# The second MoE: an earlier weight split and a second fixed slot for the second early expert

## The chip, the cores and the metric

One Trainium2 chip, one of its cores. The metric is the device time of one execution in microseconds; lower is better. The engines are TensorE (PE, matmul; its weight loads are shown as PEld), VectorE (DVE), ScalarE (ACT), GpSimd (POOL) and SyncE (SP); each has its own in-order queue, and DMAs are issued from the queues of ACT, SP and POOL.

## The reference

Clustered attention, a dense MoE layer, and a routed MoE layer. The work that is changed lies in the last one.

```
x = attn(q, k, v, centroids)                     # 2 x 8 heads, 768 tokens each, head size 64 -> [1536, 512]
x = (s * relu(x @ w_in)**2 + b) @ w_out           # 512 -> 2048 -> 512
logits = x @ w_gate                               # 8 experts
e = argmax(logits);  gate = softmax(logits)[e]
out[t] = gate[t] * (relu(x[t] @ w1[e]) @ w2[e])   # w1: 512 x 1024, w2: 1024 x 512, float32
```

## The kernel before

float32 products are made of float16 pairs: an operand is split into hi and lo parts, and three matmuls (hi·hi, hi·lo, lo·hi) are summed. So the weights of an expert, 4 MiB of float32, must be loaded into the four staging tiles stg0 to stg3 (1 MiB each; two for w1, two for w2) and split into a *set* of float16 tiles: ACT writes the hi part (L598), DVE the lo part from it (L599), in eight pieces of 128x1024 on each engine. There are three sets: `wa`, and the tiles `wi` and `wo`, which hold the dense layer's weights until these are done with.

The first MoE ends with a router: each token's row is scattered to the region of its expert in `yreg` (DRAM). The second MoE then works in *slots* of 128 rows of one expert. A slot is a gather of rows by POOL (L636), a transposing DMA by SP (L640, tile x2t), gemm1 with 96 matmuls of 128 columns (L659) into two PSUM halves hps, for each half a relu on ACT (L663) and the lo part on DVE (L664), gemm2 with 24 matmuls of 512 columns (L673), a scaling on ACT (L678, tile o) and a scatter by POOL (L679). The names below are in the order of execution:

- T0, T1, T2: three slots of the expert that has most tokens when the last quarter of the tokens is not yet routed (set wa). They are laid beside the end of the first MoE.
- H1, H2, H3: a fourth slot of that expert (wa), one of expert 1 (wi) and one of expert 0 (wo); `FIRST = (1, 0)` are the two early experts, whose weights are loaded without waiting for the routing (`w_static`, on ACT's queue). Experts 1 and 0 are fixed in the program, the expert of T and H1 and all counts come from the data.
- D0 to D9: ten dynamic slots, on wa, wi, wo in turn. What they work on (expert, rows) is computed by DVE when all tokens are routed, by some 40 small instructions that end with `idx` (L809). Their weights are loaded by SP (L625 and L630); a load is left out at run time where the expert is that of the slot ahead, since the staging tiles still hold it. The split is made again for each slot.
- `USUAL = 10, 11` (L67): ten slots are unconditional; one more stands in a conditional block, the last five of 16 in a block inside it. These run only if the count of slots needed, n_left, is over 10.

The staging tiles have one buffer each, so the load of the next expert's piece waits for the DVE split of that piece. In program order a slot j is followed by the w1 split for slot j+3 (`split(j + 3, 0, ...)`, placed after relu and lo of slot j) and by the w2 split for slot j+2 (`split(j + 2, 1, ...)`, placed after the scaling o of the slot ahead). Which instruction stands where in each engine's queue is settled when the kernel is built, by a scheduler with its own model of durations; it knows nothing of loads that are left out at run time. `tc.issue_after(x)` puts what follows behind x on x's own engine.

The weights of expert 0 are split into wo (L810 and L811) behind two instructions: `st8["relu"]`, the last relu of T2, on ACT, and `idx`, the end of the index computation, on DVE.

Of the kernel before, what the change touches and what calls it, by code (L numbers as in the profile page):

```python
# [7 lines left out]
F32 = mybir.dt.float32  # L8
F16 = mybir.dt.float16
I32 = mybir.dt.int32  # L10
U32 = mybir.dt.uint32
AF = mybir.ActivationFunctionType
ALU = mybir.AluOpType
# [12 lines left out]
SW = 64.0  # L26
# [17 lines left out]
def tile_kernel(ctx: ExitStack, tc, q, k, v, centroids, w_in, w_out, s, b, w_gate, w1, w2, out, dbg=None):  # L44
    nc = tc.nc
# [5 lines left out]
    P = 128  # L51
# [9 lines left out]
    NF = 3  # L61
# [5 lines left out]
    USUAL = 10, 11  # L67
# [524 lines left out]
    def w_split(ws, parts=range(4)):  # L592
        for i in parts:
            hi = ws[:, 2 * (i // 2), (i % 2) * 2048:(i % 2 + 1) * 2048]
            lo = ws[:, 2 * (i // 2) + 1, (i % 2) * 2048:(i % 2 + 1) * 2048]
            for n in range(2):
                a, z = n * 1024, (n + 1) * 1024
                st8["hi"] = nc.scalar.activation(out=hi[:, a:z], in_=stg[i][:, a:z], func=AF.Copy, scale=SW)  # L598
                nc.vector.scalar_tensor_tensor(out=lo[:, a:z], in0=stg[i][:, a:z], scalar=SW, in1=hi[:, a:z],  # L599
                                               op0=ALU.mult, op1=ALU.subtract)  # L600
# [10 lines left out]
    NG = 3  # L611
# [99 lines left out]
    for e in FIRST:  # L711
        nc.vector.tensor_scalar(out=done[:, e:e + 1], in0=done[:, e:e + 1], scalar1=float(P), scalar2=None, op0=ALU.add)
# [20 lines left out]
    hts = [gemm1(sets[0], pre[0][0], (st8["py"], st8["py"])), gemm1(sets[0], pre[1][0], (st8["py"], st8["ps8"]))]  # L733

# [9 lines left out]
    sinv = sp.tile([P, E], F32, name="sinv")  # L744
    sidx = sp.tile([P, E], I32, name="sidx")
    nc.vector.tensor_tensor(out=sinv, in0=doner, in1=nps, op=ALU.is_ge)
    nc.vector.tensor_scalar(out=sinv, in0=sinv, scalar1=OOB, scalar2=None, op0=ALU.mult)
    last = nc.vector.tensor_tensor(out=sidx, in0=doneg, in1=sinv, op=ALU.add)
# [7 lines left out]
    fst = [(pidxi, pinv)] + [(sidx[:, e:e + 1], sinv[:, e:e + 1]) for e in FIRST]  # L756
    fst = [fetch(ygs[(NF + n) % NG], *x) for n, x in enumerate(fst)]
# [52 lines left out]
    with tc.issue_after(st8["relu"].ins), tc.issue_after(last.ins):  # L810
        w_split(sets[2])  # L811
# [4 lines left out]
    def slots(j0, j1, head):  # L816
# [20 lines left out]
        xts = {j: fst[j + len(fst)] for j in head}  # L837
# [12 lines left out]
        for j in (*head, *range(j0, j1)):  # L850
            xt, gate, oid = xts.pop(j)
            ht = gemm1(sets[j % 3], xt)
            if due[1] > j0:
                load(due[1], 2)
            split(j + 3, 0, st8["relu"], st8["hlo"])
            if pend is not None:
                gemm2(*pend)
            split(j + 2, 1, *([st8["o"]] if "o" in st8 else []))
# [5 lines left out]
    slots(0, USUAL[0], range(-len(fst), 0))  # L864
# [29 lines left out]
```

## Time and profile before

| what | value |
|---|---|
| three runs | 734.92, 737.85, 738.41 us (median 737.85) |
| the profiled execution | 740.1 us, of which its span is 738.4 us |
| PE busy | 654.7 us, 89% of the span |
| DVE, ACT, POOL busy | 525.0, 436.2, 293.5 us |
| DMA | 98.33 MB, 133 GB/s over the span |

The page gives busy times and their share in 40 slices of the span; the timeline gives each engine's instructions in order, merged where alike, with the idle time ahead of each and what released it. Times of the trace count from the span's start. The second MoE's slots take the span from about 540 us to its end.

### The profile page before, as it was taken

How to read it: one execution, taken by the hardware profiler on the slowest of the kernel's cores; microseconds unless marked ns; L12 is line 12 of the kernel's file. 1: busy time of each engine (PE TensorE's matmuls, PEld its weight loads, DVE VectorE, ACT ScalarE, POOL GpSimd, SP SyncE). 2: the span in 40 equal slices, each digit the busy share in tenths (PEclk: the TensorE clock that was granted, in tenths of full speed). 3: DMA queues.
4: the chain of work that ended last, by engine and by line, in shares of the span. 5: the costliest groups of instructions: out<-in, count | busy, mean ns of one | idle time of the engine just before them, and what ended most of it. 6: DMA issues, size and time to landing. Idle time of an engine off the chain costs nothing. (4 is left out here: it accounts for less than half of the span.)

```text
span 738.4 us, 16238 instructions
## 1 busy us (share of the span) xinstructions
PE 654.7 (89%) x6261; PEld 426.1 (58%) x6261; DVE 525.0 (71%) x1109; ACT 436.2 (59%) x897; POOL 293.5 (40%) x336
## 2 busy tenths in 40 slices
PE   2487888898877889999999999999999999998884
PEld 2255666676544545666655654565485776675651
DVE  7999798776899976588832661377844768777672
ACT  6477676777676745567734450156514568667562
POOL 6448576656666564644433300020013234331001
PEclk9998689999899999999999999999999999999898
DMA  8967666662563604430113400038933588789821
GB/s 235 185 158 154 146 169 145 154 133 54 141 158 95 150 25 99 107 70 7 34 13 67 85 15 1 15 110 260 373 101 100 127 270 270 163 270 255 258 101 52
DMA packets 122963, 98.33 MB, mean 133 GB/s; under 512 B 98812, under 2 KB 104956, under 8 KB 120576
## 3 DMA queue, kind: packets, MB, share of 16 engines
q1 hardware_dynamic: 112784, 65.64, 36.5%
q10 hardware_dynamic: 6576, 22.06, 9.4%
q0 software_dynamic: 3520, 9.54, 3.8%
q8 instruction: 51, 0.84, 0.5%
q14 instruction: 32, 0.26, 0.1%
HBM read 85.05 MB, written 7.39 MB: 125 GB/s over the span
## 5 line engine op out<-in xcount | busy, mean ns | idle before, releaser
L291 POOL TENSOR_TENSOR pl<-p,ph 128x384 f16<-128x384 f32 x128 | 128.4, 1011 | 116.4 <-ACT ph L288 58.7
L435 PE MATMUL ps<-xt,wi 128*128 128x384 f16 x768 | 135.3, 330 | 5.7 <-DMA xt<-xp 4.1
L449 PE MATMUL py<-wo,g 128*128 128x512 f16 x576 | 132.2, 382 | 0.0
L283 ACT ACTIVATE p<-st 128x384 f32<-128x384 f32 x192 | 94.1, 491 | 52.5 <-PE st L280 41.8
L242 DVE TENSOR_REDUCE mxt<-sm 128x1 f32<-128x384 f32 x192 | 102.3, 546 | 25.1 <-PE sm L239 24.5
L435 PEld LDWEIGHTS <-wi 128*128 128x128 f16 x768 | 74.5, 99 | 56.2 <-issue 10.4
L449 PEld LDWEIGHTS <-g 128*128 128x128 f16 x576 | 55.2, 98 | 64.0 <-issue 3.7
L239 PE MATMUL sm<-tk 80*128 80x384 f16 x192 | 64.5, 363 | 17.1 <-DVE mxt L242 11.9
L278 PE MATMUL st<-tk 128*128 128x384 f16 x192 | 65.6, 342 | 7.4 <-ACT ph L288 4.6
L288 ACT ACTIVATE ph<-st 128x384 f16<-128x384 f32 x144 | 70.9, 492 | 1.1 <-PE pv L270 1.1
L679 POOL DMA_INDIRECT out<-o,oid x16 | 26.9, 1682 | 103.4 <-ACT o L678 94.6
L280 PE MATMUL st<-qb,tk 128*128 128x384 f16 x192 | 65.8, 343 | 0.0
L673 PEld LDWEIGHTS <-ht 128*128 128x128 f16 x384 | 36.8, 98 | 44.5 <-issue 3.3
L441 ACT ACTIVATE g<-r,b 128x384 f16<-128x384 f32 x64 | 39.4, 618 | 37.1 <-DVE r L440 36.8
L442 DVE SCALAR_TENSOR_TENSOR g<-r,b,g 128x384 f16<-128x384 f32 x64 | 44.8, 701 | 21.3 <-ACT g L441 21.3
L270 PEld LDWEIGHTS <-ph 128*128 128x128 f16 x864 | 45.0, 99 | 20.9 <-issue 4.2
L270 PE MATMUL pv<-v,ph 128*128 128x65 f16 x864 | 52.0, 195 | 5.4 <-ACT ph L288 3.2
L516 POOL DMA_INDIRECT yreg<-yp,posi x12 | 12.8, 1069 | 106.6 <-DVE posi L502 86.1
L599 DVE SCALAR_TENSOR_TENSOR wa<-stg,wa 128x1024 f16<-128x1024 f32 x40 | 46.8, 1218 | 7.7 <-ACT wa L598 7.6
L659 PE MATMUL hps<-x2t,wa 128*128 128x128 f16 x768 | 45.7, 219 | 3.8 <-DVE wa L599 1.5
L659 PEld LDWEIGHTS <-wa 128*128 128x128 f16 x768 | 43.7, 98 | 6.8 <-issue 2.0
L440 DVE SCALAR_TENSOR_TENSOR r<-r,s 128x384 f32<-128x384 f32 x64 | 43.4, 678 | 4.2 <-ACT r L438 4.0
(216 smaller groups left out, 1248.0 us busy)
## 6 DMA issues: line engine op xcount, KB each, us to landing
stg<-in_moe_w SPq DMA_DIRECT2D x44, 1024.0 KB
raw<-in_moe_w_out ACTq DMA_DIRECT2D x16, 512.0 KB
stg<-in_moe_w ACTq DMA_DIRECT2D x8, 1024.0 KB
raw<-in_moe_w_in ACTq DMA_DIRECT2D x10, 512.0 KB
kqv<-in_k SPq DMA_DIRECT2D x16, 192.0 KB
kqv<-in_q SPq DMA_DIRECT2D x16, 192.0 KB
kqv<-in_v SPq DMA_DIRECT2D x16, 192.0 KB
raw<-in_moe_w_in SPq DMA_DIRECT2D x6, 512.0 KB
```

Source lines behind the costliest of these rows:

```text
L239: nc.tensor.matmul(out=sm, lhsT=tk2[0:64 + C, 1, c0 + c, :], rhs=tk2[0:64 + C, 0, n * HC:(n + 1) * HC, :].rearrange("p c x -> p (c x)"), s ...
L242: nc.vector.tensor_reduce(out=mxt[:, c, n:n + 1], in_=sm, axis=AX.X, op=ALU.max)
L270: nc.tensor.matmul(out=pv[:, c, :], lhsT=p[:, c * P:(c + 1) * P], rhs=w, start=first[0], stop=(kc == NC - 1 and c == HC - 1 and p is parts ...
L278: nc.tensor.matmul(out=st.rearrange("p (c x) -> p c x", c=HC), lhsT=tk1[:, kc, 0, :], rhs=tk1[:, c0:c0 + HC, 1, :], start=True, stop=False)
L280: nc.tensor.matmul(out=st, lhsT=tk2[:, 0, kc, :], rhs=qb.rearrange("p c x -> p (c x)"), start=False, stop=True)
L283: nc.scalar.activation(out=p32, in_=st, func=AF.Exp, scale=1.0 / 8.0)
L288: nc.scalar.activation(out=ph, in_=st, func=AF.Exp, scale=1.0 / 8.0)
L291: eng.tensor_tensor(out=pl, in0=p32, in1=ph, op=ALU.subtract)
L435: nc.tensor.matmul(out=ps, lhsT=wi[:, a, kk, f * P:(f + 1) * P], rhs=xt[:, c, kk], start=(kk == 0 and n == 0), stop=(kk == KD - 1 and n == 2))
L449: st8["py"] = nc.tensor.matmul(out=ps, lhsT=g[:, a, f, c * P:(c + 1) * P], rhs=wo[:, w, f], start=(f == 0 and n == 0), stop=(f == KF - 1 a ...
L599: nc.vector.scalar_tensor_tensor(out=lo[:, a:z], in0=stg[i][:, a:z], scalar=SW, in1=hi[:, a:z], op0=ALU.mult, op1=ALU.subtract)
L659: nc.tensor.matmul(out=ps[:, j], lhsT=ws[:, w, kk * F + f0:kk * F + f0 + P], rhs=xt[:, a, kk], start=(i == 0), stop=(i == 3 * KD - 1))
```

## The change

The split of expert 0's weights is traced with two separate orders: its ACT half comes behind the last relu of T1 (`early`), its DVE half behind `idx` as before. The gathers of the H slots are traced after it. Expert 0 gets two fixed slots in a row on the same set wo: H3 with its first 128 rows (in the code -4, the `twin`) and H4 with rows 128 to 255 (in the code -1); no split is traced behind H3 for the slot three further on, since H4 needs none. `done`, from which the table of dynamic slots is made, is raised by 128 more for expert 0. `USUAL` becomes 9, 11: nine dynamic slots D0 to D8 unconditional, two in the first conditional block, five in the second.

```diff
-    USUAL = 10, 11
+    USUAL = 9, 11
@@
-    def w_split(ws, parts=range(4)):
+    def w_split(ws, parts=range(4), hi_after=None, lo_after=None):
...
-                st8["hi"] = nc.scalar.activation(out=hi[:, a:z], in_=stg[i][:, a:z], func=AF.Copy, scale=SW)
-                nc.vector.scalar_tensor_tensor(out=lo[:, a:z], in0=stg[i][:, a:z], scalar=SW, in1=hi[:, a:z],
-                                               op0=ALU.mult, op1=ALU.subtract)
+                with tc.issue_after(hi_after.ins) if hi_after else nullcontext():
+                    nc.scalar.activation(out=hi[:, a:z], in_=stg[i][:, a:z], func=AF.Copy, scale=SW)
+                with tc.issue_after(lo_after.ins) if lo_after else nullcontext():
+                    nc.vector.scalar_tensor_tensor(out=lo[:, a:z], in0=stg[i][:, a:z], scalar=SW, in1=hi[:, a:z],
+                                                   op0=ALU.mult, op1=ALU.subtract)
@@
-    for e in FIRST:
+    second = sp.tile([P, E], F32, name="second")
+    nc.vector.tensor_scalar(out=second, in0=doner, scalar1=float(P), scalar2=None, op0=ALU.add)
+    secondg = sp.tile([P, E], F32, name="secondg")
+    nc.vector.tensor_scalar(out=secondg, in0=doneg, scalar1=float(P), scalar2=None, op0=ALU.add)
+    for e in (*FIRST, FIRST[-1]):
@@
+    early = st8["relu"]
@@
-    nc.vector.tensor_tensor(out=sinv, in0=doner, in1=nps, op=ALU.is_ge)
+    nc.vector.tensor_tensor(out=sinv[:, 0], in0=doner, in1=nps, op=ALU.is_ge)
+    nc.vector.tensor_tensor(out=sinv[:, 1], in0=second, in1=nps, op=ALU.is_ge)
...
-    last = nc.vector.tensor_tensor(out=sidx, in0=doneg, in1=sinv, op=ALU.add)
+    nc.vector.tensor_tensor(out=sidx[:, 0], in0=doneg, in1=sinv[:, 0], op=ALU.add)
+    nc.vector.tensor_tensor(out=sidx[:, 1], in0=secondg, in1=sinv[:, 1], op=ALU.add)
@@
-    with tc.issue_after(st8["relu"].ins), tc.issue_after(last.ins):
-        w_split(sets[2])
+    w_split(sets[2], hi_after=early, lo_after=last)
+
+    fst = [(pidxi, pinv)] + [(sidx[:, n, e:e + 1], sinv[:, n, e:e + 1]) for n, e in ((0, FIRST[0]), (0, FIRST[1]), (1, FIRST[1]))]
+    fst = [fetch(ygs[(NF + n) % NG], *x) for n, x in enumerate(fst)]
@@
+            twin = j == -4
...
-            split(j + 3, 0, st8["relu"], st8["hlo"])
+            if not twin:
+                split(j + 3, 0, st8["relu"], st8["hlo"])
...
-            split(j + 2, 1, *([st8["o"]] if "o" in st8 else []))
+            if j != -1:
+                split((-1 if twin else j) + 2, 1, *([st8["o"]] if "o" in st8 else []))
@@
-    slots(0, USUAL[0], range(-len(fst), 0))
+    slots(0, USUAL[0], (-3, -2, -4, -1))
```

How the instructions then stand in the queues shows at three places. In the rows a number behind a name tells buffers apart, `wo` is the set of expert 0, and `x2` means two pieces.

ACT, from the relus of T1 on. Before:

```order
L663 ACTIVATE ht_8435<-hps_8436 128x512
L663 ACTIVATE ht_8435<-hps_8487 128x512
L663 ACTIVATE ht_8540<-hps_8541 128x512
L663 ACTIVATE ht_8540<-hps_8592 128x512
L678 ACTIVATE o_8668<-yps_8643,gate_7671 128x512
L598 ACTIVATE wo_2954<-stg0_6974 128x1024 x2
L598 ACTIVATE wo_2954<-stg1_6975 128x1024 x2
L598 ACTIVATE wo_2954<-stg2_6976 128x1024 x2
L598 ACTIVATE wo_2954<-stg3_6977 128x1024 x2
L678 ACTIVATE o_8698<-yps_8673,gate_7680 128x512
```

The same place now:

```order
L665 ACTIVATE ht_8440<-hps_8441 128x512
L665 ACTIVATE ht_8440<-hps_8492 128x512
L599 ACTIVATE wo_2954<-stg0_6974 128x1024 x2
L599 ACTIVATE wo_2954<-stg1_6975 128x1024 x2
L599 ACTIVATE wo_2954<-stg2_6976 128x1024 x2
L599 ACTIVATE wo_2954<-stg3_6977 128x1024 x2
L665 ACTIVATE ht_8545<-hps_8546 128x512
L665 ACTIVATE ht_8545<-hps_8597 128x512
L680 ACTIVATE o_8673<-yps_8648,gate_7676 128x512
L680 ACTIVATE o_8703<-yps_8678,gate_7685 128x512
```

The eight hi splits moved from behind T2's relus and T0's scaling to right behind T1's relus.

DVE, from the last index instructions on; yg0 to yg2 are the three gather buffers in turn, and ht_8540 (ht_8545) is T2's. Before:

```order
L809 TENSOR_TENSOR idx_8837<-t3_8838,inv_8834 128x16
L642 TENSOR_SCALAR gate_9356<-yg0_6993 128x1
L645 TENSOR_TENSOR oid_9358<-yg0_6993,inv_8834 128x1
L664 SCALAR_TENSOR_TENSOR ht_8540<-hps_8541,ht_8540 128x512
L642 TENSOR_SCALAR gate_9536<-yg1_6995 128x1
L645 TENSOR_TENSOR oid_9538<-yg1_6995,inv_8834 128x1
L664 SCALAR_TENSOR_TENSOR ht_8540<-hps_8592,ht_8540 128x512
L599 SCALAR_TENSOR_TENSOR wo_2954<-stg0_6974,wo_2954 128x1024 x2
L599 SCALAR_TENSOR_TENSOR wo_2954<-stg1_6975,wo_2954 128x1024 x2
L599 SCALAR_TENSOR_TENSOR wo_2954<-stg2_6976,wo_2954 128x1024 x2
L599 SCALAR_TENSOR_TENSOR wo_2954<-stg3_6977,wo_2954 128x1024 x2
```

Now:

```order
L816 TENSOR_TENSOR idx_8817<-t3_8818,inv_8814 128x16
L601 SCALAR_TENSOR_TENSOR wo_2954<-stg0_6974,wo_2954 128x1024 x2
L601 SCALAR_TENSOR_TENSOR wo_2954<-stg1_6975,wo_2954 128x1024 x2
L601 SCALAR_TENSOR_TENSOR wo_2954<-stg2_6976,wo_2954 128x1024
L647 TENSOR_TENSOR oid_8853<-yg1_6995,sinv_8758 128x1
L644 TENSOR_SCALAR gate_8860<-yg2_6997 128x1
L601 SCALAR_TENSOR_TENSOR wo_2954<-stg2_6976,wo_2954 128x1024
L647 TENSOR_TENSOR oid_8862<-yg2_6997,sinv_8758 128x1
L601 SCALAR_TENSOR_TENSOR wo_2954<-stg3_6977,wo_2954 128x1024 x2
L644 TENSOR_SCALAR gate_8869<-yg0_6993 128x1
L647 TENSOR_TENSOR oid_8871<-yg0_6993,sinv_8758 128x1
L666 SCALAR_TENSOR_TENSOR ht_8545<-hps_8546,ht_8545 128x512
```

The eight lo splits moved ahead of T2's two lo instructions, which now stand behind the splits and behind the gate of the fourth gather (yg0, the second rows of expert 0); behind them comes the gate of D0's gather.

ACT at the end of the slots: the last dynamic slots' splits against the scalings o. Before, from the first piece of D8's w1 (wo, stg0) to that of D9's (wa, stg0 and stg1):

```order
L598 ACTIVATE wo_2954<-stg0_6974 128x1024 x2
L678 ACTIVATE o_10729<-yps_10704,gate_10436 128x512
L598 ACTIVATE wo_2954<-stg1_6975 128x1024 x2
L598 ACTIVATE wi_73<-stg2_6976 128x1024 x2
L663 ACTIVATE ht_10751<-hps_10752 128x512
L598 ACTIVATE wi_73<-stg3_6977 128x1024 x2
L663 ACTIVATE ht_10751<-hps_10803 128x512
L598 ACTIVATE wa_6978<-stg0_6974 128x1024 x2
L678 ACTIVATE o_10879<-yps_10854,gate_10596 128x512
L598 ACTIVATE wa_6978<-stg1_6975 128x1024 x2
```

Now, from the relus of D7 to the scaling of D7; D8 is the last unconditional slot:

```order
L665 ACTIVATE ht_10720<-hps_10721 128x512
L665 ACTIVATE ht_10720<-hps_10772 128x512
L599 ACTIVATE wo_2954<-stg0_6974 128x1024 x2
L599 ACTIVATE wo_2954<-stg1_6975 128x1024 x2
L680 ACTIVATE o_10848<-yps_10823,gate_10565 128x512
L599 ACTIVATE wi_73<-stg2_6976 128x1024 x2
L665 ACTIVATE ht_10862<-hps_10863 128x512
L599 ACTIVATE wi_73<-stg3_6977 128x1024 x2
L665 ACTIVATE ht_10862<-hps_10914 128x512
L599 ACTIVATE wo_2954<-stg2_6976 128x1024 x2
L680 ACTIVATE o_10990<-yps_10965,gate_10716 128x512
L599 ACTIVATE wo_2954<-stg3_6977 128x1024 x2
```

Before, the scaling o stands between the two pieces of the w1 split of D8 and of D9 (and of D7, not shown); now both pieces of D8's w1 stand ahead of it, and a scaling stands only between the two pieces of D8's w2.

## Rows read from the trace of the kernel before

**Rows 1.** Busy time by stretch: engines, granted clock, DMA share, GB/s; the late slots.

```profile
680.00:700.00 20.00, 16.06 (x151) 12.29 (x152) 15.12 (x14) 12.28 (x15) 1.40 (x2) 0.83 0.84 261
```

**Rows 2.** Timeline of PE, a regular pair: start, us, group; the next gemm1's start.

```profile
657.15 5.52 PE L659 MATMUL hps<-x2t,wo 128*128 128x128 f16 x96
...
667.69 5.52 PE L659 MATMUL hps<-x2t,wa 128*128 128x128 f16 x96
```

**Rows 3.** Timeline of PE, slots D7, D8, D9 to the last matmuls.

```profile
678.23 0.83 PE L659 MATMUL hps<-x2t,wi 128*128 128x128 f16 x12
680.17 0.40 PE L659 MATMUL hps<-x2t,wi 128*128 128x128 f16 x4 [1.10 <-ACT wi L598]
...
682.57 5.93 PE L659 MATMUL hps<-x2t,wi 128*128 128x128 f16 x74 [0.63 <-DVE wi L599]
688.34 5.34 PE L673 MATMUL yps<-wa,ht 128*128 128x512 f16 x24
693.51 0.83 PE L659 MATMUL hps<-x2t,wo 128*128 128x128 f16 x12
...
702.98 5.34 PE L673 MATMUL yps<-wi,ht 128*128 128x512 f16 x24
708.16 0.83 PE L659 MATMUL hps<-x2t,wa 128*128 128x128 f16 x12
...
716.64 5.34 PE L673 MATMUL yps<-wo,ht 128*128 128x512 f16 x24
...
726.41 2.53 PE L673 MATMUL yps<-wa,ht 128*128 128x512 f16 x11 [0.88 <-DVE wa L599]
```

**Rows 4.** Timeline of PE, T2's gemm2 and two earlier waits.

```profile
569.05 5.34 PE L673 MATMUL yps<-wa,ht 128*128 128x512 f16 x24
...
580.29 5.52 PE L659 MATMUL hps<-x2t,wi 128*128 128x128 f16 x96 [0.70 <-DVE ht L664]
...
613.90 5.71 PE L659 MATMUL hps<-x2t,wi 128*128 128x128 f16 x96 [1.13 <-DVE ht L664]
```

**Rows 5.** Timeline of ACT while PE starts D7.

```profile
678.48 0.69 ACT L678 ACTIVATE o<-yps,gate 128x512 f32<-128x512 f32 x1 [2.43 <-issue]
679.07 1.99 ACT L598 ACTIVATE wi<-stg 128x1024 f16<-128x1024 f32 x2
```

**Rows 6.** Timeline of ACT ahead of the split of expert 0.

```profile
563.66 1.09 ACT L663 ACTIVATE ht<-hps 128x512 f16<-128x512 f32 x2 [10.42 <-PE yps L673]
...
565.21 7.68 ACT L598 ACTIVATE wo<-stg 128x1024 f16<-128x1024 f32 x8
```

**Rows 7.** Timeline of DVE from idx to the split of expert 0.

```profile
561.43 0.17 DVE L809 TENSOR_TENSOR idx<-t,inv 128x16 int32<-128x16 f32 x1
...
568.15 0.68 DVE L664 SCALAR_TENSOR_TENSOR ht<-hps,ht 128x512 f16<-128x512 f32 x1
...
570.47 9.16 DVE L599 SCALAR_TENSOR_TENSOR wo<-stg,wo 128x1024 f16<-128x1024 f32 x8
```

**Rows 8.** Timeline of POOL, gathers and scatters, and of DVE, a gather's landing.

```profile
565.16 1.00 POOL L636 DMA_INDIRECT yg<-yreg,idx  x1 [6.71 <-DMA x2t<-yg]
...
577.35 1.99 POOL L679 DMA_INDIRECT out<-o,oid  x1 [2.52 <-DMA out<-o,oid]
585.51 1.24 POOL L636 DMA_INDIRECT yg<-yreg,idx  x1 [6.17 <-DMA x2t<-yg]
...
616.96 5.17 POOL L679 DMA_INDIRECT out<-o,oid  x1 [11.17 <-ACT o L678]
...
591.99 0.15 DVE L642 TENSOR_SCALAR gate<-yg 128x1 f32<-128x1 f32 x1 [4.82 <-DMA yg<-yreg,idx]
```

**Rows 9.** DMA: SP's first weight issue, its stretch (as rows 1), a queue's MB from 560.

```profile
572.85 2.35 SPq L625 DMA_DIRECT2D stg<-in_moe_w  x2
...
572.80:580.00 7.20, 6.78 (x101) 5.84 (x100) 7.20 (x8) 2.33 (x5) 3.08 (x2) 1.00 0.11 42
...
q1 hardware_dynamic: 21792, 28.58, 54.9%
```

More of the change, by code (lines that the diff above doesn't have):

```diff
@@ L742, in tile_kernel @@
     w_static(FIRST[1])
-    sinv = sp.tile([P, E], F32, name="sinv")
-    sidx = sp.tile([P, E], I32, name="sidx")
-    nc.vector.tensor_tensor(out=sinv, in0=doner, in1=nps, op=ALU.is_ge)
+    sinv = sp.tile([P, 2, E], F32, name="sinv")
+    sidx = sp.tile([P, 2, E], I32, name="sidx")
+    nc.vector.tensor_tensor(out=sinv[:, 0], in0=doner, in1=nps, op=ALU.is_ge)
+    nc.vector.tensor_tensor(out=sinv[:, 1], in0=second, in1=nps, op=ALU.is_ge)
     nc.vector.tensor_scalar(out=sinv, in0=sinv, scalar1=OOB, scalar2=None, op0=ALU.mult)
-    last = nc.vector.tensor_tensor(out=sidx, in0=doneg, in1=sinv, op=ALU.add)
+    nc.vector.tensor_tensor(out=sidx[:, 0], in0=doneg, in1=sinv[:, 0], op=ALU.add)
+    nc.vector.tensor_tensor(out=sidx[:, 1], in0=secondg, in1=sinv[:, 1], op=ALU.add)
     nc.vector.tensor_tensor(out=tsel, in0=tone, in1=nps, op=ALU.mult)
@@ L755, in tile_kernel @@
     nc.vector.tensor_tensor(out=pidxi, in0=pidx, in1=pinv, op=ALU.add)
-    fst = [(pidxi, pinv)] + [(sidx[:, e:e + 1], sinv[:, e:e + 1]) for e in FIRST]
-    fst = [fetch(ygs[(NF + n) % NG], *x) for n, x in enumerate(fst)]
     ne = sp.tile([P, E], F32, name="ne")
@@ L836, in slots @@
         lds, due = {}, [j0, j0]
-        xts = {j: fst[j + len(fst)] for j in head}
+        xts = {j: fst[n] for n, j in enumerate(head)}
         load(j0, 0)
```

## The prediction, made before the changed kernel ran

> **What bounds the kernel now.** I read the stretches first. In the last quarter PE is busy nearly all the time except between 680 and 720 us, where it falls to 16.06 of 20 us and the granted clock to a mean of 0.83 [rows 1]: in part of it the lower of its two levels, 1.2 GHz, was granted. So the question is what PE waits for there; other engines' busy shares do not matter by themselves.
>
> Then the timeline of PE. An unhindered slot costs PE 10.54 us, from one gemm1 to the next [rows 2]; a gemm2 takes 5.17 of it (688.34 to 693.51 [rows 3]), so gemm1 takes 5.37. Against that, D7 needs 688.34 - 678.23 = 10.11 us for its gemm1, D8 702.98 - 693.51 = 9.47, D9 716.64 - 708.16 = 8.48 [rows 3]. That is 4.74 + 4.10 + 3.11 = 11.95 us lost. The last gemm2 starts at 716.64 + 5.17 = 721.81 and ends at 726.41 + 2.53 = 728.94: 7.13 us against 5.34, 1.79 lost. Together 13.74 us. The rows say why: D7 runs 12 matmuls, which need the first piece of w1, and then waits for a hi split on ACT and for lo splits on DVE [rows 3]. On ACT that hi split stands behind a scaling o, which waits for a gemm2 of PE: it starts at 678.48, after PE has already begun D7, and the split follows at 679.07 [rows 5]. So it is not a load that is late. It is a fixed place in ACT's queue: the scaling of D5 stands between the two pieces of D7's w1, and likewise for D8 and D9. Part of the loss is the clock: D7's last 74 matmuls take 5.93 us [rows 3], although 96 take 5.52 where nothing waits [rows 2].
>
> How much is there in all? From gemm2 of T2 at 569.05 [rows 4] to 728.94 PE takes 159.89 us. The work in it is 13 slots at 10.54 and one gemm2 more at 5.34, less 0.17 for three matmuls already issued: 142.2. So 17.7 us are waits and slow matmuls: 13.74 at the end and 4.0 ahead of it, of which rows 4 shows two, 0.70 and 1.13, both on the lo part of a slot ahead that stands behind splits on DVE.
>
> **Part 1: the number of slots.** Before there are 3 + 3 + 10 slots, now 3 + 4 + 9. The matmuls that run are the same, so PE's work stays at 142.2. This holds if no conditional slot runs. Before, none ran: the count of slots needed was 10 or less. Expert 0 needs exactly one dynamic slot: D0 was split from weights that lay in the staging tiles already, since from the first issue of SP at 572.85 to 580 only 42 GB/s x 7.2 us = 0.3 MB moved [rows 9], less than one piece of 1.05 MB; that happens only if D0's expert is 0. And queue q1 moved 28.58 MB from 560 on [rows 9]; 13 transposes of 128 x 1024 x 2 bytes are 3.41, the rest is 25.17 MB, six times 4.19 MB, so the other nine slots hold six experts. That expert 0 needs no second dynamic slot the rows leave open; the reference's argmax over its own inputs gives it 163 tokens, 128 in H3 and 35 in D0. So the second fixed slot takes over D0 and nine remain, which is the new limit, and the same six loads. The conditional code is longer and does not run; I cost it at nothing.
>
> What falls away is one split, D0's: eight pieces on ACT and on DVE, 7.68 and 9.16 us [rows 6, 7]. DVE and ACT are not the bound, so this by itself is worth nothing on the path; it leaves room in the queues.
>
> **Part 2: the late slots.** In the new order both pieces of D8's w1 stand directly behind the relus of D7 on ACT and ahead of the scaling of D6, so they run while PE does gemm2 of D6. The two pieces of D7's w1 stand around D6's relus, also ahead of the scaling of D5. The 11.95 us of the three gemm1 go. What is next late is DVE: after D7's gemm1 come its relu and lo (some 0.6, since two take 1.09 [rows 6], and 0.68 [rows 7]), then four lo pieces at 9.16 / 8 = 1.145, together 5.86 us against 5.17 of gemm2: **0.7** lost. In w2 of D8 the scaling still stands between the two pieces, as for D9 before; I take the same **1.8**. Its lower bound is 0.2, if the load for it is now in time: scaling, hi and lo piece take 0.6 + 1.0 + 1.2 = 2.8 us, and the 12 matmuls ahead 2.6. Nothing excludes the upper. Since the waits are shorter, the clock should stay at its upper level (2.4 GHz), as it does at the earlier waits of up to 1.13 us, where the next gemm1 takes 5.71 [rows 4].
>
> **Part 3: the early split.** ACT has 10.42 us of idle time ahead of 563.66, where T2's relus wait for PE to release a buffer, and the split of expert 0 takes 7.68 [rows 6]. The hi pieces go into that hole, and I cost them at nothing: before, ACT took them at 565.21 without waiting for a load. When the weights land the rows do not show; were it only at 563.66, the pieces would end at 571.3, T2's relu and lo follow at 572.6, and the wait below would be 0.1 longer. On DVE the lo pieces now start after idx at 561.43 plus some 0.2 for the three added index instructions, and stand ahead of T2's lo. They last 9.16, with 0.2 for small ones between: 570.96. Then comes the gate of H4's gather. That gather is issued at 565.16 as the fourth one is now; with weight loads under way, which start once the first staging tile is free at some 564, a gather took 591.99 - 585.51 = 6.48 us to land [rows 8]: 571.64. Gate and oid follow with 0.15 (the gate alone [rows 8]), then lo with 0.68 [rows 7]: 572.47. PE comes to gemm2 of T2 at 569.05, runs two matmuls (0.43) that need only hi, and waits from 569.48: **3.0 us, a new wait**. Its bounds are 2.3 (only the lo pieces) and 8.8 (rival 1). In return the wait of 0.70 ahead of H2 goes [rows 4], since H1's lo no longer stands behind the eight pieces. SP can send the first real load when the first two lo pieces are done, at about 564, and not at 580 or later: 16 us ahead for the same 25.17 MB. Of the other 3.3 us of early waits I keep one of 1.13 [rows 4]: gathers, transposes and loads still share the DMA engines, and a slot's lo still stands behind splits that wait for a load.
>
> The six small index instructions, the sixteen gates and oids (same number) and the seventh early gather (a dynamic one before) lie on DVE and POOL beside PE's work; at 0.15 us or less each I cost them at nothing beyond the 0.2 above.
>
> **Sum.** 17.7 removed, less 3.0 + 0.7 + 1.8 + 1.1 = 6.6: a gain of **11.1 us**. The profiled execution took 740.1 us, 2.25 more than the median of the runs; 740.1 would become 729.0, its span 727.3, and the median 737.85 becomes **726.7**.
>
> Two gathers now lie under the block of lo pieces. While DVE ran such pieces one POOL instruction took 5.17 us and another 1.99, where 1.0 to 1.24 is usual [rows 8]. The Trainium skill, SBUF — State Buffer, "Who interferes with whom", says that a VectorE instruction with two SBUF inputs, which the lo split is, contends with a GpSimd instruction that reads SBUF, and that the later one is blocked until the first has finished. The 5.17 agrees with it, the 1.99 in the middle of such a block only in part. If the block holds a gather through all its pieces, the time is that of the first rival.
>
> **The rivals.**
> (1) *The gather of H4 is held until the lo block ends.* POOL would be free at 570.96, the gather lands 6.48 later at 577.44, T2's lo is ready at 578.3, and PE waits 8.8 instead of 3.0: gain 5.3, **732.6**. For it: the 5.17 [rows 8]. Against it: 577.35 lies under the block that starts at 570.47 and took 1.99 only.
> (2) *Loads become the bound of the late slots.* Then about half of the 11.95 comes back, 6.0: **732.7**. For it: the DMA share of 0.84 between 680 and 700 [rows 1]. Against: ACT's row shows the queue place and not a load as the cause, and the loads start earlier.
> (3) *The gain does not arrive*: the order says one thing, but a queue elsewhere gives back the 11 us: **about 737**. Nothing in the order speaks for it.
> (4) *Slower: a tenth slot is needed.* Then the conditional block runs, two slots behind a branch with nothing prefetched: load of 4.19 MB at 261 GB/s, 16 us, a split of 9.2 and 2 x 10.54 on PE: some 46 us on top of 726.7, **773**. It decides from one row of any expert beyond its last full 128. Against: the count above, from two rows and from the reference.
>
> **How the numbers follow.** Forecast 0.62, rival 1 0.17, rival 2 0.10, rival 3 0.08, rival 4 0.03. The forecast's own bounds are losses of 2.3 + 0.2 + 0.2 + 0 = 2.7 (gain 15.0, 722.9) and of 5 + 1 + 1.8 + 3.3 = 11 (gain 6.6, 731.2). Below that I add 1.4, since the three runs shown spread by 3.5. The range that holds 8 in 10 takes in the first two rivals in good part: **721.5 to 733**. A measurement here can tell about 0.5%, 3.7 us, from no change. Faster by more (below 734.2): 0.88; within: 0.08; slower: 0.04.
>
> **What would show it.** On PE: gemm1 of D7 and D8 in 5.4 to 6.1 us with no waits on ACT; a clock near 1.00 from 680 on; a wait of about 3 us inside gemm2 of T2, on DVE's lo; 16 slots and no conditional one. On ACT: eight hi pieces of wo between 553 and 561. On SP: the first weight pieces moving at about 564. I am wrong if PE stands still inside T2 for more than 6 us, if the late gemm1 wait for a DMA, or if PE's slots between 580 and 680 cost more than 10.54 each.

## The result

Seven runs each on one chip: before 737.85 us (732.45 to 742.29), after 730.12 us (728.00 to 734.13). The ratio is 0.9899, 95% interval 0.9867 to 0.9931, so 7.5 us faster, between 5.1 and 9.8. In a second comparison (experiments below) it was 0.9922 (0.9889 to 0.9954), 5.8 us. The forecast was a gain of 11.1 us, 726.7. The sign and the range (721.5 to 733) hold; the gain is 3.6 to 5.3 us smaller than the forecast's. The ratios leave out single runs more than 1.5% above the fastest of their kernel.

Single runs of one kernel spread by up to 13 us, much of it ahead of the second MoE, where nothing was changed: in the thirteen profiles of this document the matmul of the counts (`nps`) starts anywhere between 547.02 and 556.73. So beside each ratio I give a length from the trace: from `nps` (L736 before, L743 after) to the end of PE's last matmul. Before it is 728.94 - 552.03 = 176.9 us, after 718.63 - 549.44 = 169.2: 7.7 us less. Such a length is that of one profiled run; for the kernel after, profiled twice, it is 169.2 and 172.0, so a difference of 3 us or less between two kernels shows nothing without the rows behind it.

The windows of the kernel after (columns: us, then busy time and count of PE, PEld, DVE, ACT, POOL, granted clock, DMA share, GB/s):

```profile
560.00:580.00 20.00, 16.33 (x123) 9.16 (x122) 9.83 (x17) 3.63 (x6) 6.87 (x4) 0.91 0.80 271
580.00:600.00 20.00, 16.98 (x231) 13.75 (x229) 10.88 (x16) 14.20 (x17) 4.80 (x4) 1.00 0.69 176
600.00:680.00 80.00, 80.00 (x892) 57.56 (x890) 61.35 (x73) 51.48 (x63) 17.22 (x13) 1.00 0.78 225
680.00:700.00 20.00, 20.00 (x230) 14.57 (x228) 15.64 (x16) 14.65 (x18) 1.99 (x2) 1.00 0.67 204
700.00:728.00 28.00, 16.80 (x147) 10.09 (x145) 12.24 (x12) 10.81 (x13) 3.39 (x3) 0.92 0.25 92
```

The stretch from 680 to 700 us, 16.06 us busy at 0.83 before [rows 1], is now full at 1.00. The idle time is in two stretches ahead of 600 and at the end. PE's timeline of the kernel after shows where (start, duration, operation, count; in brackets the idle time ahead and what ended it):

```profile
549.44 0.17 PE L743 MATMUL nps<-acc,ones 128*128 128x8 f16 x1
...
555.04 10.74 PE L675 MATMUL yps<-wa,ht 128*128 128x512 f16 x49
569.45 4.45 PE L675 MATMUL yps<-wa,ht 128*128 128x512 f16 x12 [3.67 <-DVE ht L666]
...
595.41 5.52 PE L661 MATMUL hps<-x2t,wo 128*128 128x128 f16 x96 [3.02 <-DVE ht L666]
...
689.83 5.52 PE L661 MATMUL hps<-x2t,wi 128*128 128x128 f16 x96
695.19 5.34 PE L675 MATMUL yps<-wa,ht 128*128 128x512 f16 x24
700.37 5.59 PE L661 MATMUL hps<-x2t,wo 128*128 128x128 f16 x96
705.80 5.34 PE L675 MATMUL yps<-wi,ht 128*128 128x512 f16 x24
711.24 0.38 PE L675 MATMUL yps<-wo,ht 128*128 128x512 f16 x1
712.50 2.75 PE L675 MATMUL yps<-wo,ht 128*128 128x512 f16 x12 [0.88 <-DVE wo L601]
716.10 2.53 PE L675 MATMUL yps<-wo,ht 128*128 128x512 f16 x11 [0.85 <-DVE wo L601]
```

These answer [rows 3, 4]. D7 and D8 go from slot to slot in 10.54 (689.83 to 700.37), as an unhindered slot does [rows 2]; the 11.95 us are gone. New are two waits: in T2's gemm2 (3.67, and behind it 12 matmuls in 4.45 where they cost 2.59 at the upper clock, so 1.86 more; together 5.5 us, from 565.61, when PE has done the two matmuls of T2 that need only hi, to 573.73, with 2.59 of work), and ahead of H3's gemm1 (3.02; its product buffer comes free with H2's lo). The last gemm2 lasts from 710.98 to 718.63, 7.65 against 5.34. By the same count as in the prediction: T2's gemm2 begins at 565.18 (with the last two of the 49 matmuls), PE ends at 718.63, 153.45 us with 142.36 of work (13 slots at 10.54 and one gemm2 at 5.34): 11.1 lost, against 17.7. The sum had 6.6.

DVE's timeline of the kernel after says what the two waits stand behind:

```profile
557.90 0.15 DVE L644 TENSOR_SCALAR gate<-yg 128x1 f32<-128x1 f32 x1 [2.91 <-DMA yg<-yreg,pidxi]
...
558.10 0.17 DVE L816 TENSOR_TENSOR idx<-t,inv 128x16 int32<-128x16 f32 x1
558.18 5.76 DVE L601 SCALAR_TENSOR_TENSOR wo<-stg,wo 128x1024 f16<-128x1024 f32 x5
...
568.57 0.15 DVE L644 TENSOR_SCALAR gate<-yg 128x1 f32<-128x1 f32 x1 [0.98 <-DMA yg<-yreg,sidx]
...
568.70 1.28 DVE L666 SCALAR_TENSOR_TENSOR ht<-hps,ht 128x512 f16<-128x512 f32 x2
...
594.53 0.15 DVE L644 TENSOR_SCALAR gate<-yg 128x1 f32<-128x1 f32 x1 [6.88 <-DMA yg<-yreg,idx]
...
594.67 1.28 DVE L666 SCALAR_TENSOR_TENSOR ht<-hps,ht 128x512 f16<-128x512 f32 x2
```

Three times DVE stands still at a gate whose gather has not landed: ahead of idx and so of the whole block of lo pieces (2.91; it stood there before, too, with 3.16 in its trace), ahead of T2's lo (0.98), and ahead of H2's lo (6.88, the sixth gather, that of D1). In the kernel before the gate of the sixth gather, there D2's, stands behind H2's lo (591.99 [rows 8]), so it held no lo of H2:

```profile
585.74 1.42 DVE L664 SCALAR_TENSOR_TENSOR ht<-hps,ht 128x512 f16<-128x512 f32 x2
```

The gate itself takes 0.15 and its result is not needed before the slot's scaling; what stands behind it in DVE's queue is what PE waits for.

### The profile page after: what moved, and what is told of

The parts are those of the page before. It is cut to its first block, busy times and chain, and to the rows that moved or that the text cites. A ratio compares the mean times of both kernels' runs of the same rounds, so it can differ in the third digit from the quotient of the medians.

```text
span 728.1 us, 16197 instructions
## 1 busy us (share of the span) xinstructions
PE 649.9 (89%) x6261; PEld 423.6 (58%) x6261; DVE 516.2 (71%) x1106; ACT 429.4 (59%) x889; POOL 286.1 (39%) x336
## 4 chain that ended last, share of the span: by engine, by line
PE 43%; DMA 15%; DVE 9%; issue 7%; ACT 2%; POOL 0%; POOLq 0%; ACTq 0%; DVEq 0%; SPq 0%
PE py L449 15%; PE ps L435 13%; DMA out<-o,oid 6%; PE hps L661 5%; PE yps L675 3%; PE pv L270 2%; DMA x2t<-yg 1%; DVE r L440 1%; DVE g L442 1%; DMA tk<-pk 1%; DMA raw<-in_moe_w_out 1%; PE sm L239 1%; PE st L278 1%; DVE mxt L242 1%; DMA yg<-yreg,idx 1%
## 5 line engine op out<-in xcount | busy, mean ns | idle before, releaser
L435 PE MATMUL ps<-xt,wi 128*128 128x384 f16 x768 | 136.9, 333 | 5.7 <-DMA xt<-xp 4.1
L449 PE MATMUL py<-wo,g 128*128 128x512 f16 x576 | 130.6, 379 | 0.0
L681 POOL DMA_INDIRECT out<-o,oid x16 | 19.6, 1224 | 79.4 <-ACT o L680 68.5
L601 DVE SCALAR_TENSOR_TENSOR wo<-stg,wo 128x1024 f16<-128x1024 f32 x32 | 37.4, 1218 | 13.3 <-ACT wo L599 13.3
L270 PE MATMUL pv<-vw,p 128*128 128x65 f32 x288 | 44.5, 295 | 0.0
L270 PE MATMUL pv<-v,pl 128*128 128x65 f16 x432 | 38.2, 196 | 5.3 <-POOL pl L291 2.8
```

Of the source, the lines that this page charges most:

```text
L270: nc.tensor.matmul(out=pv[:, c, :], lhsT=p[:, c * P:(c + 1) * P], rhs=w, start=first[0], stop=(kc == NC - 1 and c == HC - 1 and p is parts ...
L435: nc.tensor.matmul(out=ps, lhsT=wi[:, a, kk, f * P:(f + 1) * P], rhs=xt[:, c, kk], start=(kk == 0 and n == 0), stop=(kk == KD - 1 and n == 2))
L449: st8["py"] = nc.tensor.matmul(out=ps, lhsT=g[:, a, f, c * P:(c + 1) * P], rhs=wo[:, w, f], start=(f == 0 and n == 0), stop=(f == KF - 1 a ...
```

## The experiments

Each kernel was run six or twelve times in rounds beside the kernel before, on three chips: the rows from "early split alone" to "gates late (first form)" on one, "after, again" and the three rows from "after, gates late" on the second, the last three rows on the third. Times are compared on one chip, ratios across chips. "PE length" is the one defined above. Half of a weight (w1 or w2) lies in one staging tile and is two pieces; "between the pieces of w1" means between its halves.

| kernel | ratio to before (95%) | PE length |
|---|---|---|
| before | 1 | 176.9 |
| after | 0.9899 (0.9867 to 0.9931) | 169.2 |
| after, again | 0.9922 (0.9889 to 0.9954) | 172.0 |
| early split alone | 1.0004 (0.9971 to 1.0037) | 182.9 |
| second fixed slot alone | 0.9887 (0.9842 to 0.9931) | 173.0 |
| before, scaling behind w1 | 0.9935 (0.9900 to 0.9971) | 170.2 |
| after, gates late (first form) | 0.9846 (0.9783 to 0.9909) | 167.5 |
| after, gates late | 0.9870 (0.9826 to 0.9914) | 165.7 |
| after, scaling behind w2 | 0.9985 (0.9957 to 1.0013) | 173.7 |
| gates late, scaling behind w1 and w2 | 0.9873 (0.9823 to 0.9922) | 166.2 |
| the same, D8's relus behind w2 | 0.9882 (0.9832 to 0.9933) | 163.7 |
| gates late, scaling behind w1 | 0.9805 (0.9753 to 0.9856) | 163.5 |
| gates late, without the early split | 0.9930 (0.9893 to 0.9967) | 168.0 |

### The early split alone

In the kernel before, only the split of expert 0 moves, and the early gathers are traced behind it; the slots stay 3 + 3 + 10.

```diff
...
-    with tc.issue_after(st8["relu"].ins), tc.issue_after(last.ins):
-        w_split(sets[2])
+    w_split(sets[2], hi_after=early, lo_after=last)
...
```

> The kernel before with the early split alone: expert 0's pieces are split from the hole ahead of T2's relus on, as in the kernel after, but the slots stay 3 + 3 + 10. Theory A (the late slots' gain comes from where the scaling o stands on ACT, and the early split only costs): D7 to D9 still lose some 12 us at their first matmuls with the scaling between the two pieces of w1, and PE waits 3.0 to 5.5 us at T2, as the kernel after does (a wait of 3.67 and 12 matmuls in 4.45 instead of 2.59); the time is 737.9 + 3.0 to 5.5 - 0.7 = 740 to 743, slower than before. Theory B (the early split, with loads that start sooner, is what gains): faster than before by 4 us or more, at most 734.

The ratio is 1.0004, so B falls: the early split does not carry the gain. A's net loss, 2.3 to 4.8 us, is hardly in the times either, whose interval ends at 1.0037, 2.7 us. PE's timeline of this kernel shows A's waits (the profiled run was the slowest of its twelve, 746.25 us against a median of 741.59):

```profile
571.68 4.21 PE L675 MATMUL yps<-wa,ht 128*128 128x512 f16 x12 [1.97 <-DVE ht L666]
...
598.30 8.01 PE L661 MATMUL hps<-x2t,wo 128*128 128x128 f16 x96 [3.69 <-DVE ht L666]
...
700.21 0.83 PE L661 MATMUL hps<-x2t,wo 128*128 128x128 f16 x12
702.14 0.40 PE L661 MATMUL hps<-x2t,wo 128*128 128x128 f16 x4 [1.10 <-ACT wo L599]
```

The two early waits stand at the places of those in the kernel after. At T2 it is 1.97 and not 3.67: here DVE stands at no gate ahead of T2's lo, it works through the lo pieces without idle time, so this is the cost of the place behind them (the block itself still starts behind the gate ahead of idx). D8 (as D7 and D9) still waits as in [rows 3]; the three lose 10.6 us.

### The second fixed slot alone

In the kernel after, expert 0 is split where the kernel before does it (the diff above the other way round).

> The kernel after without the early split: the second fixed slot H4 and nine dynamic slots stay, expert 0's weights are split where the kernel before splits them, behind T2's last relu and idx. Theory A: the wait at T2 (3.67, and 1.86 of slow matmuls) goes and 0.7 to 1.1 ahead of H2 comes back, the late slots stay free of ACT: 730.1 - 5.5 + 0.9 = about 725.5. Theory B (the early split pays by starting the loads 11 us sooner): the loads become late in the second half, PE waits there for them or for splits that wait for them, and the time is 731 to 737.

0.9887 is as much as the whole change gives: the gain is the slot's, or rather that of the order on ACT that the scheduler chooses with it: D7 and D8 run without a wait here as well. But A's 725.5 would have been a ratio of 0.983, and that is just outside the interval. The wait in T2 is gone, and another has come in its place, on PE and, behind it, on DVE:

```profile
606.98 7.53 PE L661 MATMUL hps<-x2t,wo 128*128 128x128 f16 x96 [6.18 <-DVE ht L666]
```

```profile
596.89 0.15 DVE L644 TENSOR_SCALAR gate<-yg 128x1 f32<-128x1 f32 x1 [12.46 <-DMA yg<-yreg,idx]
...
606.25 1.28 DVE L666 SCALAR_TENSOR_TENSOR ht<-hps,ht 128x512 f16<-128x512 f32 x2
```

DVE stands 12.46 us at the gate of a dynamic slot's gather; the splits queued behind it run until 606.25, and only then comes H3's lo, for which H4's gemm1 waits. So the gate is one cause. A late load, as B had it, is another: ACT too stands still, for more than twice as long as in the kernel after (3.62), until the load for D1's split has come, and it has H3's relu behind that split:

```profile
591.40 2.00 ACT L599 ACTIVATE wi<-stg 128x1024 f16<-128x1024 f32 x2 [8.17 <-DMA stg<-in_moe_w]
```

With no gate in the way 3.0 us of waits are left here (last experiment). By the ratio the time is 729.5 where before is 737.85, between A's 725.5 and B's 731.

### Before, with the scaling behind w1's pieces

In the kernel before, the scaling o of a slot stands on ACT behind both hi pieces of the next slot's w1.

```diff
...
+            if due[0] == j + 3 < j1:
+                split(j + 3, 0, st8["relu"], st8["hlo"])
+                w1hi[j + 3] = st8["hi"]
...
-                gemm2(*pend)
+                gemm2(*pend, after=w1hi.get(j + 1))
```

> The kernel before, and one thing more: on ACT the scaling o of each dynamic slot stands behind both hi pieces of the next slot's w1, not between them. Nothing else is moved by hand, the slots are 3 + 3 + 10. Theory A (the place of the scaling on ACT is the cause of the 11.95 us that D7 to D9 lose): D7 to D9 do their gemm1 in 5.4 to 6.2 us each, the time is 737.9 - 11.95 + 3 x 0.7 = about 728. Theory B (the loads or the splits themselves are late, and the scaling merely stands beside them): the three gemm1 still lose 2 us or more each, less than 4 us are gained, 734 or more.

Ten dynamic slots, nothing but the order on ACT changed, and the gemm1 of D7, D8 and D9 take 6.23, 7.07 and 6.22 us: of 11.95 lost, 3.4 are left, and no wait for ACT. So the place of the scaling is the cause of most of it, as A has it, though D8's 7.07 is above A's 6.2. The gain, 4.8 us by the ratio and 6.7 by PE's length, is smaller than A's 10, above all since the last gemm2, which now comes earlier, loses 5.3 where it lost 1.8:

```profile
674.77 1.46 PE L659 MATMUL hps<-x2t,wi 128*128 128x128 f16 x22
676.86 4.30 PE L659 MATMUL hps<-x2t,wi 128*128 128x128 f16 x74 [0.62 <-DVE wi L599]
681.00 5.34 PE L673 MATMUL yps<-wa,ht 128*128 128x512 f16 x24
686.18 1.17 PE L659 MATMUL hps<-x2t,wo 128*128 128x128 f16 x16
...
693.25 5.34 PE L673 MATMUL yps<-wi,ht 128*128 128x512 f16 x24
698.43 1.46 PE L659 MATMUL hps<-x2t,wa 128*128 128x128 f16 x22
...
704.65 5.34 PE L673 MATMUL yps<-wo,ht 128*128 128x512 f16 x24
709.84 3.06 PE L673 MATMUL yps<-wa,ht 128*128 128x512 f16 x12
714.98 0.38 PE L673 MATMUL yps<-wa,ht 128*128 128x512 f16 x1 [2.09 <-ACT wa L598]
716.24 4.22 PE L673 MATMUL yps<-wa,ht 128*128 128x512 f16 x11 [0.88 <-DVE wa L599]
```

On the same chip the second fixed slot alone has a median of 733.37 and this kernel, without that slot, 734.53: most of what the slot gives, moving the scalings on ACT gives too, and the intervals of the two ratios overlap.

### The gates behind the lo parts

In the kernel after, the gate and oid of the H and D slots (`meta`, now apart from the gather) are traced behind the lo part of their own slot.

```diff
...
             ht = gemm1(sets[j % 3], xt)
+            with tc.issue_after(st8["hlo"].ins):
+                gate, oid = meta(yg, einv)
```

> The kernel after, with the gate and oid of H1 to H4 and of the dynamic slots placed behind the lo part of their own slot on DVE, so that no lo part stands behind a gather that has not landed. Theory A (gates that wait for a gather hold T2's lo for the last 1 us and H2's lo for 3.02 us): the wait ahead of H3 goes, the one at T2 shrinks from 3.67 to between 2.3 and 2.9, the lo pieces alone, and with it perhaps the slow matmuls: 730.1 - 3.0 - 0.8 to 2.6 = 724.5 to 726.5. Theory B (the waits end with the lo splits, the gates are only the last of several things that are late): both waits stay within 1 us of what they are, 729 to 731.

In this first form H1 takes its factor and row numbers from H4's rows, which are gathered into the same buffer ahead of its gate, so H1's rows are not written to their places; the amount of work is the same. Both waits are gone, the one in T2 wholly, which A did not expect: idx no longer stands behind a gate either, and the block of lo pieces begins 6.1 us behind the `nps` matmul (557.96 - 551.82) instead of 8.7. At the end D8's gemm1 loses 3.1 and the last gemm2 5.2. The next form puts H1's gate right:

```diff
...
+        if n == 0:
+            with tc.issue_after(st8["hlo"].ins):
+                fst[0] = (fst[0][0], *meta(*fst[0][1:]))
```

> The kernel after once more, beside the next ones on one chip. From the first measurement (0.9899): PE's time from the matmul of the counts (nps) to its last instruction 169.2 us against 176.9 of before; waits of 3.67 at T2 with slow matmuls behind it, 3.02 ahead of H3, about 2.3 us lost in the last gemm2. Theory A (these waits are set by fixed orders on DVE and ACT): the same three waits come again within 1 us. Theory B (they are chance, from loads and gathers that land late in one run): at least one of them is gone or over 1.5 us different.

> The kernel after with the gates behind the lo parts, as in the run before, but with H1's gate read ahead of H4's gather into the same buffer, directly behind T2's lo parts, so that the whole result is computed. Theory A (gates that wait for gathers held idx, T2's lo and H2's lo): the block of lo pieces starts about 6 us behind the nps matmul instead of 8.7, no wait over 1 us at T2 and at H3; what is given back is in the last two slots, as in the run before, where the scaling stood between the two pieces of D8's w1 again (3.5 us) and the last gemm2 lost 5: from nps to PE's end 167 to 169 us, time as the kernel after or up to 3 us less. Theory B (the waits went only because H1's gate had been moved behind H4's gather): the wait at T2 or at H3 comes back, 2 us or more.

The kernel after shows its three losses again: 2.65 with the same slow 12 matmuls (4.45) in T2, 3.66 ahead of H3, this time with slow matmuls behind it (7.15 instead of 5.52), and 2.4 in the last gemm2:

```profile
570.87 4.45 PE L675 MATMUL yps<-wa,ht 128*128 128x512 f16 x12 [2.65 <-DVE ht L666]
...
597.47 7.15 PE L661 MATMUL hps<-x2t,wo 128*128 128x128 f16 x96 [3.66 <-DVE ht L666]
```

The wait at T2 is 1.02 us shorter, just over the 1 us that A allowed; that the three come again at the same places speaks for orders and against chance. With the gates late there is neither wait; T2's gemm2 runs through behind those of T0 and T1, and H3 follows H2 directly:

```profile
563.78 13.33 PE L678 MATMUL yps<-wa,ht 128*128 128x512 f16 x61
...
595.44 5.52 PE L664 MATMUL hps<-x2t,wo 128*128 128x128 f16 x96
...
702.34 0.40 PE L664 MATMUL hps<-x2t,wo 128*128 128x128 f16 x4 [1.10 <-ACT wo L599]
```

The new order of the queues put the scaling between D8's w1 pieces again (the last row), which costs 3.1 us, and still the PE length is 165.7, below the 167 to 169 expected. The mean of the six runs is 730.1 us, against 734.3 for the kernel after on the same chip.

### The end: scaling and w2

In the kernel after, for the last three slots, the scaling stands behind both hi pieces of w2 (`whi` holds the last hi piece of each split by half and slot):

```diff
...
-                gemm2(*pend)
+                gemm2(*pend, after=[whi[x] for x in ((1, j),) if x in whi and j >= j1 - 3])
```

> The kernel after, and one thing more: on ACT, for the last three slots, the scaling of the slot ahead stands behind both hi pieces of w2 (of D7 and of D8), so that the staging tiles of w2 come free sooner. Theory A (the end is set by a chain: scaling of D6 waits for PE, behind it D7's w2 is split, its tiles come free, D8's w2 is loaded in 5.5 us and split): the loads of D8's w2 land some 2 to 4 us earlier, the last gemm2 loses 0 to 1 us instead of 2.3, 1 to 2.5 us faster than the kernel after. Theory B (the loads' own rate sets the end, the tiles are free long before): D8's w2 lands when it did, the last gemm2 loses 2 us or more, no gain.

A is wrong, and B has the outcome without the reason: the kernel is not faster than the kernel after on the same chip (0.9922) but slower, 0.9985, and D8's w2 does not land when it did but later. The last gemm2 loses 6.9 us. On ACT only the first half of D7's w2 moved ahead; the second stayed behind D8's first relu. And the load of D8's last half took 8.1 us from the split that frees its tile (713.67) to its own split (721.75), against 5.9 in the kernel after (707.87 to 713.73). The DMA queues carry in this stretch, beside the loads, one scatter of 0.26 MB here and none in the kernel after, since D6's scaling, whose result it writes, now comes later. But the load took 7.7 and 8.5 us in the next two kernels and 6.5 in the one with the lowest ratio, each with such a scatter beside it, and 7.3 and 6.5 in the two kernels with the gates late, without the data of a scatter. So the scatter does not settle it: why this load took 2 us longer stays open.

The same on the version with the gates late, and behind the next slot's w1 as well:

```diff
-                gemm2(*pend)
+                gemm2(*pend, after=[whi[x] for x in ((1, j), (0, j + 1)) if x in whi and j >= j1 - 3])
```

> Gates behind the lo parts, as in the run with H1's gate put right, and for the last three slots the scaling on ACT behind both hi pieces of the next slot's w1 and of its own slot's w2. If the three causes are those named (gates on DVE; scaling between the w1 pieces; scaling ahead of w2), each wait goes and none replaces it: from nps to PE's end 162.5 to 165 us, against 169.2 of the kernel after and 176.9 of before, so 5 to 7 us faster than the kernel after and some 12 to 14 faster than before (ratio 0.981 to 0.985). If a wait only moves (loads late once PE is faster), 167 us or more and no gain over the kernel after.

The waits at T2, at H3 and at D8's w1 are gone (0.62 is left there), but the end gives 5.6 us back, so it is 166.2, between the two forecasts, and no gain over the gates alone (0.9873 against 0.9870).

To that version, D8's relus behind D7's w2:

```diff
-            ht = gemm1(sets[j % 3], xt)
+            ht = gemm1(sets[j % 3], xt, relu_after=whi.get((1, j - 1)) if j == j1 - 1 else None)
```

> The version with the gates late and the scaling behind w1 and w2, and one thing more: D8's relus stand on ACT behind all four hi pieces of D7's w2, ahead of which only D8's w1 is split. In the version without it the second half of D7's w2 was split behind D8's first relu, at 697.45, and the load of D8's second half of w2 began at 700.92 and landed at 708.59, 1.3 us after PE wanted it. Theory A (the chain at the end goes over the staging tile: split of D7's w2, load of D8's w2, split): that load begins 1.7 to 2.9 us sooner, the last gemm2 loses 1 to 3 us instead of 5.6, from nps to PE's end 162.5 to 164.5 us against 166.2. Theory B (the load itself is slow at the end, whatever its start): it lands no earlier relative to PE's last gemm2, 166 us or more.

PE's length falls to 163.7, as A has it. By itself a fall of 2.5 us would show nothing, but the rows go with it: the tile comes free sooner (second half split by 697.36, that is 6.6 us behind the start of D8's gemm1 at 690.72 against 8.4 before), the last gemm2 loses 3.2 us instead of 5.6. The ratio is 0.9882, no better; the six runs spread by 13 us (722.16, the profiled one, to 735.44), with what lies ahead of the second MoE in them.

The gates late, and the scaling behind w1 alone:

```diff
-                gemm2(*pend)
+                gemm2(*pend, after=[whi[x] for x in ((0, j + 1),) if x in whi and j >= j1 - 3])
```

> Gates late, and on ACT only the scaling of D6 and of D7's two forerunners behind both hi pieces of the next slot's w1; the splits of w2 stay where the scheduler puts them. Theory A (the place of the scaling between w1's pieces costs D8's gemm1 3.3 us whenever the order has it there): D8's gemm1 takes 5.4 to 6.2 us instead of 8.5, and the last gemm2, which then comes earlier than its w2, loses 1 to 3 us more than the 3.2 it lost before: from nps to PE's end 164 to 166 us against 165.7. Theory B: D8's gemm1 takes 8 us or more all the same.

D8's gemm1 takes 6.36 us instead of 8.5, somewhat more than A's 6.2, so the place of the scaling is the cause here too. A's other half missed: the last gemm2 loses 3.0, no more than before. This gives 163.5 and a ratio of 0.9805 (0.9753 to 0.9856), whose interval lies below both intervals of the kernel after. It is the lowest ratio of all, but not clear of that of the kernel just before (0.9832 to 0.9933), whose PE length is the same, nor of the gates late alone. PE's last rows of it:

```profile
697.93 4.30 PE L664 MATMUL hps<-x2t,wo 128*128 128x128 f16 x74 [0.63 <-DVE wo L601]
702.07 5.34 PE L678 MATMUL yps<-wi,ht 128*128 128x512 f16 x24
707.25 0.38 PE L678 MATMUL yps<-wo,ht 128*128 128x512 f16 x1
708.48 2.53 PE L678 MATMUL yps<-wo,ht 128*128 128x512 f16 x11 [0.85 <-DVE wo L601]
711.84 0.38 PE L678 MATMUL yps<-wo,ht 128*128 128x512 f16 x1 [0.82 <-ACT wo L599]
713.10 2.53 PE L678 MATMUL yps<-wo,ht 128*128 128x512 f16 x11 [0.88 <-DVE wo L601]
```

### What the early split is worth with the gates out of the way

> The kernel with gates late, but expert 0 split where the kernel before splits it, behind T2's last relu and idx: second fixed slot without the early split, no gate ahead of a lo part. Theory A (with the gates out of the way the early split is worth little, since both orders leave PE without a wait at T2 and the loads have time): from nps to PE's end within 1.5 us of the 165.7 of the version with the early split, time within 2 us of it. Theory B (the early split starts the loads some 10 us sooner and that is needed): PE waits for loads or for splits that wait for loads between H2 and D3, 3 us or more.

The edit is that of the second fixed slot alone, on the version with the gates late. 168.0 against 165.7, and 0.9930 against 0.9870 (the intervals overlap). PE waits 1.33 and 1.71 us at H3 and H4, 3.0 together, where the version with the early split does not wait; the first of these is for a relu of ACT, the second for a lo part. Both stand behind splits of D0 and D1, and ahead of that of D1 ACT stood still until a load came:

```profile
599.78 0.60 PE L678 MATMUL yps<-wo,ht 128*128 128x512 f16 x2 [1.33 <-ACT ht L668]
602.09 5.52 PE L664 MATMUL hps<-x2t,wo 128*128 128x128 f16 x96 [1.71 <-DVE ht L669]
```

```profile
590.98 2.00 ACT L599 ACTIVATE wi<-stg 128x1024 f16<-128x1024 f32 x2 [7.62 <-DMA stg<-in_moe_w]
```

So B's mechanism is there, at the edge of its size: with the early split, whose loads start sooner, these 3.0 us do not arise. That it is worth time is not shown: the 2.3 us in PE length are within what two profiles of one kernel differ by, and the two ratios, from two chips, overlap.

## Why the prediction came out as it did

**The late slots** were right, in cause and in size: a fixed place in ACT's queue, not a load. The kernel before with that place alone changed shows it for 8.5 of the 11.95 us, and in the kernel after D7 and D8 wait nowhere (D9 is not there any more). The 0.7 for DVE's lo pieces at D8 were 0.07. The four hi pieces ran right behind D7's relus, as forecast; but the forecast had PE wait for all four lo pieces, and PE, which began D8's gemm1 at 700.37, lost next to nothing although the last of them ended only at 701.60. That the order is free at D8 is not owed to the second slot as such: in three kernels that have the slot but late gates (first form, gates late, without the early split) the scheduler put the scaling between the pieces again and D8 lost 3.1.

**The wait in T2** was forecast as 3.0 and was 3.67. The step that missed is the landing of H4's gather: in PE's time it was issued 3.2 us ahead of T2's gemm2 (562.01 against 565.18), not 3.9. Its length was right, 6.56 us (562.01 to 568.57) against 6.48, but by luck: POOL was at it for 2.81 us instead of the 1.24 of the gather in [rows 8], and from there to the gate it took 3.75 instead of 5.24. Larger than that: the slow matmuls behind the wait, 1.86 us, were not in the sum at all. The prediction priced the clock at the end, where the waits shrank, and not at the wait that the change makes. The rest of this part came as forecast: the hi pieces ran in the hole (550.13 to 557.80), SP's first load was issued at 562.04, and the 0.70 ahead of H2 went.

**The mid wait** was forecast as 1.13, taken over from [rows 4] with the reason that a lo part stands behind splits that wait for a load. It was 3.02 and 3.66, and the reason was another: H2's lo stood behind the gate of the sixth gather. In the kernel before that lo stood ahead of that gate; the prediction read the order at T2 and at the end, not between. This is the largest single term of the miss; with both of its terms T2 is larger.

**The end** was forecast as 1.8 and lost 2.3 to 2.4. The forecast took over the scaling between the pieces; in fact ACT was done with that scaling at 712.71 and then waited for the load:

```profile
713.73 2.00 ACT L599 ACTIVATE wo<-stg 128x1024 f16<-128x1024 f32 x2 [1.03 <-SPq L879]
```

The second half arrives only when the tile has been freed and loaded, and most of the kernels whose PE came earlier lost more there, up to 5.6 with the gates late.

In sum: 0.67 + 1.86 + 2.1 + 0.5 - 0.6 = 4.5 us more lost than forecast (the 2.1 are 595.41 - 592.22, when PE had done its last matmuls ahead of the mid wait, less 1.1), and 11.1 - 4.5 = 6.6 is what is left from T2's gemm2 on (17.7 - 11.1). PE's length fell by 7.7: another 1.1 us went between `nps` and T2's gemm2, for which the forecast had no term. The times show 7.5 and 5.8.

**Rival 1**, H4's gather held through the whole block of lo pieces: the gather stood on POOL for 2.81 us in the middle of that block (POOL's timeline: issued at 562.01) and was out before the block ended at 567.6:

```profile
562.01 2.81 POOL L638 DMA_INDIRECT yg<-yreg,sidx  x1 [6.49 <-DVE wo L601]
565.13 0.99 POOL L638 DMA_INDIRECT yg<-yreg,idx  x1 [0.30 <-issue]
```

The Trainium skill, SBUF — State Buffer, "Who interferes with whom", has the port that the two share as an exclusive lock, so that the later waits for the first. The trace agrees in part: 2.81 is longer than the 1.0 of an undisturbed gather and near the length of two pieces, and the next gather, inside the same block, took 0.99. So in these rows a gather is held for a piece or two, and not each time; in the second fixed slot alone one (at 603.51) took 3.71 among four such pieces. The hold may have cost something: the 0.98 us for which T2's lo stood at the gate is less than the 1.8 by which POOL took longer. No run shows it by itself.

**Rival 2**, loads that bound the late slots, did not come in those slots. In the last gemm2 it did, in a form that the prediction did not name: a chain over the staging tile, split, load, split. **Rivals 3 and 4** fell: there are nine dynamic slots and no conditional one.

## What to carry to other kernels

A small instruction that waits for a DMA holds all that is behind it in its engine's queue: before a move is priced, look for such waits (here a gate of 0.15 us behind a gather) between the moved work and its consumer, in the new order, along the whole stretch and not only at the move itself. Of a wait that a change makes on PE, price the slow matmuls behind it too. Where a scheduler settles the order of the queues, read it again after every change: an order that was free can come back. At the end of a loop with a fixed number of staging tiles look at the chain of split, load and split: whatever makes the engine ahead of it faster meets it next.

## What the runs showed that I had not expected

A wait's length alone does not say whether the clock falls behind it. Behind 3.67 us in T2 the 12 matmuls took 4.45 instead of 2.59 (window clock 0.91), behind 1.97 us at the same place 4.21; but behind the 3.02 us ahead of H3 all 96 took 5.52, the full rate (granted clock 1.00), while in another run of the same kernel 3.66 us there made them 7.15, and 3.69 in the early split alone 8.01.

The load of the last half of w2 (1.05 MB), from the freed tile to its split, took between 5.9 us (the kernel after) and 8.5 (D8's relus behind w2); the cause of the difference was not found.
